# More exponentials moved from ScalarE to VectorE: a cheaper polynomial, its exponent bits on GpSimd, and a searched plan

## The chip, the cores and the metric

The kernel runs on one core of one Trainium2 chip. The metric is the device time of one execution in microseconds. All quoted runs are in the fast state unless said otherwise; executions of one kernel agree within 0.7%, those of e4 below within 1.1%. Names: PE is TensorE (matmul), PEld its weight load, ACT is ScalarE, DVE is VectorE, POOL is GpSimd. SBUF is the on-chip memory for operands, PSUM the one for TensorE's results. The *granted clock* is the share of full speed at which TensorE was allowed to run, as the profile records it.

## The reference

Two attention branches over the same `x` (2048 x 512, 32 heads of 16) are mixed by a gate. Branch A is softmax attention, branch B linear attention with softmax features.

```python
scores = jnp.einsum("bhqd,bhkd->bhqk", q, k) * (Dh ** -0.5)
p = softmax(scores)                       # 32 x 2048 x 2048 exponentials: this sets the time
a = (p @ v) @ wo
phi = concat(softmax(q @ w_phi), softmax(-q @ w_phi))   # branch B, small
b = (phi_q @ (phi_k^T v)) / (phi_q @ sum(phi_k)) @ wo
out = g * a + (1 - g) * b                 # g = sigmoid(x . gate_w)
```

Branch A's exponentials are cut into 2048 *units* of 128 x 512 (128 keys, 512 queries, one head). ScalarE does most of them. Some are done on VectorE, four units (four heads, one key tile) at a time: a *pack*.

## The kernel before

The program orders itself when it is built: every instruction is an `Op` with an engine, a duration, a priority and an earliest time, and a list scheduler turns them into one fixed order per engine. On the chip each engine runs its list in order and waits on semaphores. So "the plan" below means these fixed orders.

The work is 32 stretches of four heads and 512 queries. How many packs each gives to VectorE, and which key tiles they are:

```python
DVE_COUNT = (1, 2, 1, 1, 1, 2, 1, 2, 2, 1, 2, 2, 1, 2, 2, 2, 1, 2, 2, 1, 2, 2, 2, 1, 2, 2, 2, 1, 2, 3, 2, 2)   # 54
def dve_tiles(n):
    return ((6,), (5, 11), (4, 8, 12))[DVE_COUNT[min(n, NN - 1)] - 1]
```

The main chain on ScalarE takes three and two units at a time out of a ring of five PSUM banks:

```python
o_exp = s.op("act", w * 0.434 + 0.045, lambda e: e.activation(ET[:, s0:s0 + w, :], ps_ring[:, b0:b0 + w, :], ACT.Exp, scale=...))
```

A pack on VectorE writes `x*log2(e)` in fixed point (16 bits of fraction), then builds the bits of the bfloat16 result: 128 times the fixed-point number plus a correction, a polynomial in the fraction.

```python
rel = a + (z - a) * (j / nj) - 14 if n else a + 6     # when the pack's scores may be made
pr = rel + 12                                         # its priority
for i in range(4):      # scores into one of two PSUM banks, then a conversion out of it
    m = s.op("pe", ...matmul(self.bk(b), kT, qT))
    ws.append(s.op("dve", 0.605, ...tensor_scalar(EW[.., i], self.bk(b), EC, 127 * 65536, op0=mult, op1=add)))
f  = tensor_scalar(Ef, low_half(EW), 2.0 ** -16)      # f16 fraction, strided read
m1 = tensor_scalar(Em, Ef, 1.0, subtract)
t  = tensor_scalar(Et, Ef, 128 * EB, 128 * (EA - EB / 2), mult, add)
u  = tensor_tensor(Em, Ef, Em, mult)
g_ = tensor_tensor(Et, Et, Em, mult)
for hf in range(2):     # merge: reads the int32 words again
    scalar_tensor_tensor(ED[.., hf], in0=EW[.., hf], scalar=2.0 ** -9, in1=Et[.., hf], mult, add)
# ... TensorE then multiplies ED by V into the same accumulator as ScalarE's units
```

The softmax here doesn't subtract the row's maximum and nothing guards it: scores larger than these inputs give would overflow.

## Time and profile before

The time is 896.4 us (median of three runs; 895.56 to 900.07). The profiled run spans 897.3 us.

| what | us | read from |
|---|---|---|
| ACT busy | 864.0 (96%) | busy line |
| main exponentials | 837.9, 1832 units | costliest groups |
| DVE busy | 753.3 (84%) | busy line |
| first main exponential starts | 12.26 | timeline of ACT |
| last one ends, to the end | 9.3 | trace, records of ACT |
| gaps of ACT between the two | 13.7 | trace, records of ACT |

The first fence has lines of the profile page of the kernel before: busy time by engine (share of the span, instruction count), the chain of work that ended last, and three of the costliest groups (line, engine, operation, output and input, count | busy us, mean ns of one | idle time just before them).

```profile
PE 777.6 (87%) x5515; PEld 216.1 (24%) x5515; DVE 753.3 (84%) x1062; ACT 864.0 (96%) x801; POOL 7.0 (1%) x11
...
ACT 85%; PE 9%; DVE 3%; SPq 2%; DMA 0%; issue 0%; ACTq 0%
...
L691 ACT ACTIVATE ET<-ps_ring 128x1536 bf16<-128x1536 f32 (+1 forms) x733 | 837.9, 1331 | 15.5 <-PE ps_ring L674 8.0
...
L768 DVE TENSOR_SCALAR EW<-ps_mp 128x512 int32<-128x512 f32 x216 | 143.2, 681 | 45.6 <-PE ps_mp L764 44.7
...
L783 DVE SCALAR_TENSOR_TENSOR ED<-EW,Et 128x1024 uint16<-128x1024 int32 x108 | 126.3, 1210 | 0.3
```

ScalarE is the limit: it is busy 96% of the span and is 85% of the chain. VectorE has room: 45.6 us of its idle time lies before the conversions. The two merges of a pack are its dearest part: 126.3 us over 54 packs is 2.34 us per pack.

What one unit costs is read from the chain where it runs undisturbed. These are pieces of it (start, us, what):

```profile
466.85 22.60 ACT ET L691 x20
490.43 22.60 ACT ET L691 x20
```

Twenty instructions of three and two units alternating are 50 units, so a unit costs 22.60 / 50 = 0.452 us.

### The profile page before, as it was taken

To read this page: it belongs to the slowest core of one execution; us is meant where nothing else is said; L and a number is where in the kernel's file an instruction comes from. 1 tells how busy PE (TensorE), PEld (TensorE's weight loads), DVE (VectorE), ACT (ScalarE), POOL (GpSimd) and SP (SyncE) were. 2 spreads that over 40 slices of the span, in tenths; PEclk is the share of its full clock that TensorE was granted. 3 is DMA by queue.
4 is the path that set the end of the run, shared out by engine and by line. 5 is a ranking of instruction groups with operands and counts; after the bars stand their busy time and mean duration, and the time that the engine had idled before them with its cause. 6 is when DMAs were issued, how large, how long until landed. Compare 5 with 4: busy or idle time off the path is not lost.

```text
span 897.3 us, 13165 instructions
## 1 busy us (share of the span) xinstructions
PE 777.6 (87%) x5515; PEld 216.1 (24%) x5515; DVE 753.3 (84%) x1062; ACT 864.0 (96%) x801; POOL 7.0 (1%) x11
## 2 busy tenths in 40 slices
PE   7999998988888888888989888898888889887885
PEld 2223322222221222222222222222222222211221
DVE  3787878989994999699796897899979898889985
ACT  5998999999999999999999999999999999999985
POOL 3000000000000000000000000000000000000000
PEclk9999999999999999999999999999999999999998
DMA  5231000000000000000000000000000000000000
GB/s 111 55 76 49 1 7 3 2 4 4 4 4 1 4 4 4 4 1 10 10 10 10 4 7 10 10 7 8 1 4 4 10 10 13 6 1 4 4 1 24
DMA packets 25114, 11.21 MB, mean 12 GB/s; under 512 B 18016, under 2 KB 25056, under 8 KB 25056
## 3 DMA queue, kind: packets, MB, share of 16 engines
q1 hardware_dynamic: 23472, 9.99, 4.2%
q8 instruction: 43, 0.70, 0.3%
q10 hardware_dynamic: 1584, 0.39, 0.2%
q14 instruction: 15, 0.12, 0.0%
HBM read 3.16 MB, written 2.10 MB: 6 GB/s over the span
## 4 chain that ended last, share of the span: by engine, by line
ACT 85%; PE 9%; DVE 3%; SPq 2%; DMA 0%; issue 0%; ACTq 0%
ACT ET L691 82%; PE ps_ring L674 4%; ACT phi L913 3%; PE ps_mp L992 2%; SPq L501 2%; PE ps_ot L719 1%; PE ps_mp L561 1%; DVE ED L783 1%; DVE Em L778 0%; DVE EW L768 0%; PE ps_mp L764 0%; DMA xT<-in_A_x_dram 0%; DVE Ef L773 0%; DVE Et L779 0%; DVE Em L775 0%
## 5 line engine op out<-in xcount | busy, mean ns | idle before, releaser
L691 ACT ACTIVATE ET<-ps_ring 128x1536 bf16<-128x1536 f32 (+1 forms) x733 | 837.9, 1331 | 15.5 <-PE ps_ring L674 8.0
L674 PE MATMUL ps_ring<-qT,kT 64*128 64x512 bf16 x1832 | 365.8, 387 | 99.3 <-ACT ET L691 92.0
L768 DVE TENSOR_SCALAR EW<-ps_mp 128x512 int32<-128x512 f32 x216 | 143.2, 681 | 45.6 <-PE ps_mp L764 44.7
L719 PE MATMUL ps_ot<-ET,Vaug 128*17 128x512 bf16 x1832 | 177.4, 387 | 1.2 <-ACT ET L691 0.7
L674 PEld LDWEIGHTS ps_ring<-qT,kT 64*128 64x128 bf16 x1832 | 75.7, 93 | 334.6 <-ACT ET L691 301.9
L783 DVE SCALAR_TENSOR_TENSOR ED<-EW,Et 128x1024 uint16<-128x1024 int32 x108 | 126.3, 1210 | 0.3
L764 PE MATMUL ps_mp<-qT,kT 128*128 128x512 bf16 x216 | 79.8, 391 | 3.2 <-DVE EW L768 1.3
L719 PEld LDWEIGHTS ps_ot<-ET,Vaug 128*17 128x17 bf16 x1832 | 42.5, 87 | 139.5 <-issue 125.8
L773 DVE TENSOR_SCALAR Ef<-EW 128x2048 f16<-128x2048 uint16 x54 | 65.5, 1213 | 1.0
L778 DVE TENSOR_TENSOR Em<-Ef,Em 128x2048 f16<-128x2048 f16 x54 | 65.8, 1219 | 0.0
L779 DVE TENSOR_TENSOR Et<-Et,Em 128x2048 f16<-128x2048 f16 x54 | 65.5, 1212 | 0.3
L917 DVE TENSOR_REDUCE fsum<-phi 128x64 f32<-128x1024 bf16 x32 | 38.9, 1215 | 17.1 <-ACT phi L913 17.0
L736 PE MATMUL ps_ot<-zero,iden 128*32 128x512 bf16 (+2 forms) x288 | 47.7, 389 | 0.0
L561 PE MATMUL ps_mp<-Wp,xT 128*128 128x512 bf16 x128 | 40.3, 385 | 0.0
L561 PE MATMUL ps_mp<-xT,WA 128*128 128x512 bf16 x128 | 39.0, 385 | 1.1 <-DMA xT<-in_A_x_dram 1.1
L919 DVE TENSOR_TENSOR phi<-phi,frec 128x1024 bf16<-128x1024 bf16 x32 | 38.9, 1215 | 0.2
L913 ACT ACTIVATE phi<-ps_mp 128x512 bf16<-128x512 f32 x64 | 37.8, 699 | 0.0
L775 DVE TENSOR_SCALAR Em<-Ef 128x2048 f16<-128x2048 f16 x54 | 36.8, 681 | 0.9
L776 DVE TENSOR_SCALAR Et<-Ef 128x2048 f16<-128x2048 f16 x54 | 37.0, 685 | 0.0
L764 PEld LDWEIGHTS ps_mp<-qT,kT 128*128 128x128 bf16 x216 | 19.9, 96 | 53.5 <-issue 20.9
L802 DVE STREAM_TRANSPOSE T_80<-ps_ot 128x512 f32<-128x512 f32 x32 | 22.6, 708 | 8.1 <-PE ps_ot L719 8.1
L618 DVE CAST Vaug<-ps_mp 128x128 bf16<-128x128 f32 (+1 forms) x32 | 13.2, 424 | 14.2 <-PE ps_mp L561 14.1
(69 smaller groups left out, 405.7 us busy)
## 6 DMA issues: line engine op xcount, KB each, us to landing
out_dram<-outt SPq DMA_DIRECT2D x16, 128.0 KB, 1.7
qT<-qst SPq DMA_DIRECT2D x120, 16.0 KB, 1.8
WA<-in_A_wqkv_dram SPq DMA_DIRECT2D x3, 384.0 KB, 4.6
WBV<-in_B_wqkv_dram SPq DMA_DIRECT2D x1, 512.0 KB, 5.4
WoA<-in_A_wo_dram SPq DMA_DIRECT2D x1, 512.0 KB, 3.8
WoB<-in_B_wo_dram SPq DMA_DIRECT2D x1, 512.0 KB, 4.6
WA<-in_A_wqkv_dram ACTq DMA_DIRECT2D x3, 128.0 KB, 3.4
xT<-in_A_x_dram SPq DMA_TRANSPOSE x16, 2.7
```

The lines of the kernel that those rows point to most:

```text
L561: m = s.op("pe", self.c_mm(n), lambda e, c=c: e.matmul(self.bk(b)[:, 0:n], lhs(c), rhs(c), start=(c == 0), stop=(c == 3)), deps if c == 0 ...
L674: return lambda e: e.matmul(self.ps_ring[:, x % RING, :], self.kT[r, g // 2, kt * P:(kt + 1) * P], self.qT[r, n % 2, i, :], start=True, st ...
L691: self.o_exp.append(s.op("act", w * 0.434 + 0.045, lambda e, b0=b0, s0=s0, w=w: e.activation(self.ET[:, s0:s0 + w, :], self.ps_ring[:, b0: ...
L719: return lambda e: e.matmul(self.ps_ot[32 * i:32 * i + VSL, :], self.Vaug[:, kt, h, :], self.ET[:, (4 * p + k) % NSLOT, :], start=(kt == 0 ...
L736: return lambda e: e.matmul(self.ps_ot[c:c + nc, :], self.iden[r:r + nr, 0:nc], self.zero[r:r + nr, :], start=False, stop=False, tile_posi ...
L764: m = s.op("pe", self.c_mm(512), lambda e, i=i, b=b: e.matmul(self.bk(b), self.kT[:, cp, kt * P:(kt + 1) * P], self.qT[:, n % 2, i, :], st ...
L768: ws.append(s.op("dve", 0.605, lambda e, i=i, b=b: e.tensor_scalar(self.EW[:, ew.idx, i * QCH:(i + 1) * QCH], self.bk(b), float(EC), float ...
L773: f = s.op("dve", 1.13, lambda e: e.tensor_scalar(self.Ef[:], lo(), float(2.0 ** -16), None, op0=ALU.mult), ws + [self.ed_prev], pr)
L778: u = s.op("dve", 1.13, lambda e: e.tensor_tensor(self.Em[:], self.Ef[:], self.Em[:], ALU.mult), [m1], pr)
L779: g_ = s.op("dve", 1.13, lambda e: e.tensor_tensor(self.Et[:], self.Et[:], self.Em[:], ALU.mult), [t, u], pr)
L783: vs.append(s.op("dve", 1.12, lambda e, c0=c0: e.scalar_tensor_tensor(out=self.ED[:, ed.idx, c0], in0=self.EW[:, ew.idx, c0], scalar=float ...
L913: ex.append(s.op("act", 0.478, lambda e, sg=sg: e.activation(self.phi[:, ph.idx, :, sg, :], self.bk(b).rearrange("p (h f) -> p h f", f=DH) ...
```

## The change

The intent: make a pack cheaper for VectorE, so that it can take more packs, 65 instead of 54. The polynomial becomes a cubic about the middle of the fraction (d = f - 0.49985); its constant part is the integer 53. The exponent bits, `128 * high_half + 53`, are made by GpSimd. One 16-bit addition replaces the two int32 merges. GpSimd and VectorE can get into each other's way at the SBUF, so the plan gets two new notions: a `port` flag on VectorE instructions that it keeps apart from GpSimd's pass, and a `gate` that releases the pass of one pack only at the first or second PSUM conversion of a later one. All leads, paces and bounds are replaced by searched numbers. Three smaller edits are in the diff too: up to four packs per stretch instead of three, the score matmuls of successive packs kept in order, and a higher priority (`LEAD[2]`) for VectorE instructions that free one of the scarce PSUM banks.

```diff
+LEAD = [16.9408, 8.9394, 19.7683, 21.1253, 20.1566]
+PACE = [7.9948, 0.4589]
+BOUNDS = [5.8136, 10.5124, 10.0461, 26.2873]
-EA, EB = 0.34370964, 0.07826797
+EM = 53
+EPHI = 0.49984589
+E1, E2, E3 = 125.48413, 43.840203, 9.9574722
-DVE_COUNT = (1, 2, 1, 1, 1, 2, 1, 2, 2, ...)    # 54
+DVE_COUNT = (1, 1, 1, 2, 2, 2, 2, 1, 3, ...)    # 65
 ... (scheduler: a gated GpSimd op is parked until a gate op starts on VectorE; it then waits for the op before that one)
+            if e == "dve":
+                while o.gate and parked:
+                    c = parked.pop(0)
+                    c.war.append(last)
 ... (in the pack)
-        rel = a + (z - a) * (j / nj) - 14 if n else a + 6
-        pr = rel + 12
+        rel = a + (z - a) * (j / nj) - LEAD[0] if n else a + 6
+        pr = rel + LEAD[1]
+        h = s.op("pool", 1.9, lambda e: e.tensor_scalar(
+            out().bitcast(dt.int16), half(1, dt.int16), 128.0, float(EM), op0=ALU.mult, op1=ALU.add), ws, pr, gate=...)
-        f, m1, t, u, g_ and two scalar_tensor_tensor merges
+        f = tensor_scalar(Ef, half(0), 2.0 ** -16, -EPHI, mult, add)      # port
+        t = tensor_scalar(Em, Ef, E3, E2, mult, add)                      # port
+        u = tensor_tensor(Em, Ef, Em, mult)                               # port
+        q = tensor_scalar(Em, Em, E1, add)                                # port
+        g_ = tensor_tensor(Em, Ef, Em, mult)                              # port
+        vs = [tensor_tensor(out(), out().bitcast(int16), Em, add)]        # port; waits for h
 ... (port flags on three instructions outside the packs; LEAD, PACE, BOUNDS in place of the old constants)
```

More of the change, by code (lines that the diff above doesn't have):

```diff
@@ L28 @@
 PASSES = 1
+LEAD = [16.9408, 8.9394, 19.7683, 21.1253, 20.1566]
+PACE = [7.9948, 0.4589]
+BOUNDS = [5.8136, 10.5124, 10.0461, 26.2873]
 VSL = 17
 EC = 0.25 * 1.4426950408889634 * 65536
-EA, EB = 0.34370964, 0.07826797
-DVE_COUNT = (1, 2, 1, 1, 1, 2, 1, 2, 2, 1, 2, 2, 1, 2, 2, 2, 1, 2, 2, 1, 2, 2, 2, 1, 2, 2, 2, 1, 2, 3, 2, 2)
+EM = 53
+EPHI = 0.49984589
+E1, E2, E3 = 125.48413, 43.840203, 9.9574722
+DVE_COUNT = (1, 1, 1, 2, 2, 2, 2, 1, 3, 2, 1, 3, 1, 2, 3, 1, 2, 3, 2, 2, 2, 2, 3, 2, 1, 3, 2, 2, 4, 1, 3, 3)
 def dve_tiles(n):
-    return ((6,), (5, 11), (4, 8, 12))[DVE_COUNT[min(n, NN - 1)] - 1]
+    return ((6,), (5, 11), (4, 8, 12), (3, 6, 9, 12))[DVE_COUNT[min(n, NN - 1)] - 1]
 class Buf:
@@ L66, with __init__ @@
     __slots__ = ("eng", "dur", "fns", "deps", "prio", "rel", "alloc", "frees", "nleft", "users", "start", "end",
-                 "ready", "seq", "dma", "order", "inc", "tick", "clock", "war", "cols", "lat", "cfg", "exp", "grp")
-    def __init__(self, eng, dur, fns, deps, prio, rel, alloc, frees, dma, order, cols=0, cfg="F"):
+                 "ready", "seq", "dma", "order", "inc", "tick", "clock", "war", "cols", "lat", "cfg", "exp", "grp", "port",
+                 "gate", "go")
+    def __init__(self, eng, dur, fns, deps, prio, rel, alloc, frees, dma, order, cols=0, cfg="F", port=False,
+                 gate=False):
         self.cols = cols
+        self.port = port or eng == "pool"
+        self.gate = gate
+        self.go = False
         self.cfg = cfg
@@ L104, in op @@
     def op(self, eng, dur, fns, deps=(), prio=0.0, rel=0.0, alloc=(), frees=(), dma=0, order=(),
-           cols=0, cfg="F"):
+           cols=0, cfg="F", port=False, gate=False):
         if not isinstance(fns, (list, tuple)):
@@ L109, in op @@
             cols = 90
-        o = Op(eng, dur, list(fns), deps, prio, rel, alloc, frees, dma, order, cols, cfg)
+        o = Op(eng, dur, list(fns), deps, prio, rel, alloc, frees, dma, order, cols, cfg, port, gate)
+        if eng == "dve" and any(getattr(b.pool, "scarce", False) for b in o.frees):
+            o.prio -= LEAD[2]
         self.ops.append(o)
@@ L154, in run @@
         cfg = "F"
+        hold = {"dve": 0.0, "pool": 0.0}
+        parked, last = [], None
         self.at = 0
@@ L182, in run @@
                     best = (s, e)
+            if best is None and parked:
+                c = parked.pop(0)
+                c.go = True
+                heapq.heappush(future["pool"], (max(t.values()), c.seq, c))
+                continue
             assert best is not None, "scheduler is stuck"
@@ L210, in run @@
                         continue
+                if e == "pool" and c.gate and not c.go:
+                    parked.append(c)
+                    continue
+                if e == "dve" and c.port and hold["pool"] > now + 0.02 and len(held) < 8:
+                    held.append(it)
+                    continue
                 o = c
                 break
+            if e == "pool" and o is None:
+                continue
+            if e == "dve" and o is None and held:
+                o = held[0][2]
+                held = held[1:]
             if o is None:
@@ L238, in run @@
                 o.war.extend(war)
+            if o.port:
+                other = "dve" if e == "pool" else "pool"
+                now = max(now, hold[other])
+                hold[e] = now + o.dur
+            if e == "dve":
+                while o.gate and parked:
+                    c = parked.pop(0)
+                    c.go = True
+                    if last is not None:
+                        c.war.append(last)
+                    heapq.heappush(future["pool"], (now + self.TAIL["dve"], c.seq, c))
+                last = o
             o.start = now
@@ L419, in memory @@
         at("Em", [P, 4 * QCH], dt.float16)
-        at("Et", [P, 4 * QCH], dt.float16)
         at("ED", [P, 2, 4 * QCH], dt.uint16)
@@ L439, in pools @@
         self.mp = BufPool(2)
+        self.mp.scarce = True
         self.qst_p = BufPool(2)
@@ L468, in program @@
     def program(self):
-        self.T0 = 11.0
-        self.ut = 0.481
+        self.T0, self.ut = PACE
         self.loads()
@@ L570, in emit_qT @@
         n0 = qc * NG + 2 * cp
-        dl = self.tn(n0) - (14.0 if n0 else 2.0)
+        dl = self.tn(n0) - (LEAD[4] if n0 else 2.0)
         st = Buf(self.qst_p, 8 if n0 == 0 else 2)
@@ L580, in emit_qT @@
                     self.qT[:, n, i, :], self.qst[:, st.idx, :], self.par[:, n, i:i + 1], None, op0=ALU.mult),
-                    [o_ev, self.o_par, self.o_qz[n]], dl + 6 * n, 12 * n, frees=[st]) for i in ORDER]
+                    [o_ev, self.o_par, self.o_qz[n]], dl + 6 * n, 12 * n, frees=[st], port=True) for i in ORDER]
         self.st_q[n0 // 2] = (st, o_ev)
@@ L594, in place_qT @@
             "sp", 0.24, [put(i) for i in range(4)],
-            [o_ev, self.qk_last.get(n - 2), self.qk_dve.get(n - 2), self.o_qz[par]], self.tn(n) - 14.0, dma=65536,
+            [o_ev, self.qk_last.get(n - 2), self.qk_dve.get(n - 2), self.o_qz[par]], self.tn(n) - LEAD[4], dma=65536,
             frees=[st])]
@@ L633, in main_chain @@
             pos.append(pos[-1] + 64 - 4 * len(dve_tiles(n)))
-        self.ed_prev = None
+        self.ed_prev = self.eq_prev = None
         self.units = units
@@ L756, in dve_pack @@
         a, z = self.tn(n), self.tn(n + 1)
-        rel = a + (z - a) * (j / nj) - 14 if n else a + 6
-        pr = rel + 12
+        rel = a + (z - a) * (j / nj) - LEAD[0] if n else a + 6
+        pr = rel + LEAD[1]
         ew, ed = Buf(self.EW_p, 2), Buf(self.ED_p, 1)
         ws = []
-        m = None
+        m = self.eq_prev
         for i in range(4):
@@ L769, in dve_pack @@
                 self.EW[:, ew.idx, i * QCH:(i + 1) * QCH], self.bk(b), float(EC), float(127 * 65536),
-                op0=ALU.mult, op1=ALU.add), [m], pr, frees=[b]))
-            self.qk_dve[n] = m
-        lo = lambda: self.EW[:, ew.idx, :].bitcast(dt.uint16).rearrange("p (n two) -> p n two", two=2)[:, :, 0]
-        f = s.op("dve", 1.13, lambda e: e.tensor_scalar(self.Ef[:], lo(), float(2.0 ** -16), None, op0=ALU.mult),
-                 ws + [self.ed_prev], pr)
-        m1 = s.op("dve", 0.6, lambda e: e.tensor_scalar(self.Em[:], self.Ef[:], 1.0, None, op0=ALU.subtract), [f], pr)
@@ L776, in dve_pack @@
-        t = s.op("dve", 0.6, lambda e: e.tensor_scalar(
-            self.Et[:], self.Ef[:], float(128 * EB), float(128 * (EA - EB / 2)), op0=ALU.mult, op1=ALU.add), [f], pr)
-        u = s.op("dve", 1.13, lambda e: e.tensor_tensor(self.Em[:], self.Ef[:], self.Em[:], ALU.mult), [m1], pr)
-        g_ = s.op("dve", 1.13, lambda e: e.tensor_tensor(self.Et[:], self.Et[:], self.Em[:], ALU.mult), [t, u], pr)
-        vs = []
-        for hf in range(2):
-            c0 = slice(hf * 2 * QCH, (hf + 1) * 2 * QCH)
-            vs.append(s.op("dve", 1.12, lambda e, c0=c0: e.scalar_tensor_tensor(
-                out=self.ED[:, ed.idx, c0], in0=self.EW[:, ew.idx, c0], scalar=float(2.0 ** -9), in1=self.Et[:, c0],
-                op0=ALU.mult, op1=ALU.add), [g_], pr, alloc=[ed] if hf == 0 else (), frees=[ew],
-                order=vs[-1:]))
+                op0=ALU.mult, op1=ALU.add), [m], pr, frees=[b], gate=i < 2))
@@ new lines, in dve_pack @@
+            self.qk_dve[n] = self.eq_prev = m
+        half = lambda k, t: self.EW[:, ew.idx, :].bitcast(t).rearrange("p (n two) -> p n two", two=2)[:, :, k]
+        out = lambda: self.ED[:, ed.idx, :]
+        h = s.op("pool", 1.9, lambda e: e.tensor_scalar(
+            out().bitcast(dt.int16), half(1, dt.int16), 128.0, float(EM), op0=ALU.mult, op1=ALU.add), ws, pr,
+            alloc=[ed], frees=[ew], gate=(n, j) != (NN - 1, nj - 1))
+        f = s.op("dve", 1.13, lambda e: e.tensor_scalar(
+            self.Ef[:], half(0, dt.uint16), float(2.0 ** -16), -EPHI, op0=ALU.mult, op1=ALU.add),
+            ws + [self.ed_prev], pr, frees=[ew], port=True)
@@ new lines, in dve_pack @@
+        t = s.op("dve", 0.6, lambda e: e.tensor_scalar(
+            self.Em[:], self.Ef[:], E3, E2, op0=ALU.mult, op1=ALU.add), [f], pr, port=True)
+        u = s.op("dve", 1.13, lambda e: e.tensor_tensor(self.Em[:], self.Ef[:], self.Em[:], ALU.mult), [t], pr, port=True)
+        q = s.op("dve", 0.6, lambda e: e.tensor_scalar(self.Em[:], self.Em[:], E1, None, op0=ALU.add), [u], pr, port=True)
+        g_ = s.op("dve", 1.13, lambda e: e.tensor_tensor(self.Em[:], self.Ef[:], self.Em[:], ALU.mult), [q], pr, port=True)
@@ L787, in dve_pack @@
+        vs = [s.op("dve", 1.13, lambda e: e.tensor_tensor(out(), out().bitcast(dt.int16), self.Em[:], ALU.add), [g_, h], pr,
+                   port=True)]
         self.ed_prev = vs[-1]
@@ L809, in norm @@
             self.rinv[:, j, :, None].to_broadcast([P, 16, DH]), ALU.mult),
-            [rc, self.o_onTA.get((n - 2) // 2) if j == 0 else None], pr)
+            [rc, self.o_onTA.get((n - 2) // 2) if j == 0 else None], pr, port=True)
         if j == 0:
@@ L857, in branch_b @@
                     self.bk(b).rearrange("p (c j) -> p c j", c=4)), 512, r + 8)
-        k0, k1 = tn(3.4), tn(12.4)
-        q0, q1 = tn(13), tn(28)
+        k0, k1 = tn(BOUNDS[0]), tn(BOUNDS[1])
+        q0, q1 = tn(BOUNDS[2]), tn(BOUNDS[3])
         self.o_onTB, self.b_onTB = {}, {}
@@ L867, in branch_b @@
             b, m = self.proj(lambda c, t=t: self.xT[:, c, t * P:(t + 1) * P], lambda c: self.WBV[:, c, :], D,
-                             [self.d_wbv], r + 18, r + 4, 1, [vb])
+                             [self.d_wbv], r + 18, r + 4 - LEAD[3], 1, [vb])
             o_vb = s.op("dve", self.c_v(512), lambda e, b=b, vb=vb: e.tensor_copy(
@@ L909, in feature @@
         b, m = self.proj(lambda c: self.xT[:, c, t * P:(t + 1) * P], lambda c: self.Wp[:, c, D * qk:D * qk + D], D,
-                         [self.o_wp[(qk, jc)] for jc in range(4)], r + 5, r, 2, [ph, fs])
+                         [self.o_wp[(qk, jc)] for jc in range(4)], r + 5, r - LEAD[3], 2, [ph, fs])
         ex = []
@@ L920, in feature @@
             flat(), flat(), self.frec[:, fs.idx, :, None].to_broadcast([P, 64, DH]), ALU.mult), [rc], r + 10,
-            frees=[fs])
+            frees=[fs], port=True)
         return ph, sc
```

## The prediction

> **What bounds the kernel now.** ScalarE. The page's busy line gives ACT 864.0 of 897.3 us (96%), DVE 753.3 (84%), PE 777.6, POOL 7.0 (1%); the chain that ended last is 85% ACT, 82% the main exponentials. Those are 1832 units of 128x512, run in groups of three and two. In undisturbed stretches of the chain twenty instructions (50 units) take 22.60 us: 0.452 us per unit. The remaining 33 us of the span: 10 to 12 us before the first main exponential (it starts at 12.26), about 9 us after the last, and some 12 us of gaps between, where ACT waits for scores or for a product (the waits view: 8.0 and 6.8 us, part of it at the start).
>
> **What the change does.**
> - Offloaded packs 54 to 65: 11 x 4 = 44 units leave ScalarE. 44 x 0.452 = 19.9 us, all on the critical engine.
> - VectorE per pack, before, by starts of successive instructions in the timeline: four PSUM conversions about 2.5 us, the strided fraction 1.13, two short passes 1.2, two products 2.26, two int32 merges 2.24: about 9.4. After: 2.5 + 1.13 + 0.6 + 1.13 + 0.6 + 1.13 + one 16-bit add 1.13, about 8.2. The total goes from 54 x 9.4 = 508 to 65 x 8.2 = 533 us. VectorE then is busy about 780 us, near 89% of a shorter span; it must idle less, and can: much of its idle time is work not yet released.
> - GpSimd gets 65 passes over 2048 elements. An estimate from its 128x2048 fill in this trace (1874 ns) is 1.9 us each, about 125 us, off the chain. The danger is the port: the Trainium skill, "SBUF — State Buffer", Who interferes with whom, says that a VectorE instruction in a 2-port mode or with two SBUF inputs and a GpSimd instruction block each other whole, while one with at most one SBUF input outside these modes does not contend. This trace cannot show it: GpSimd works only at the start. The change releases each pass at the start of a later pack's PSUM conversions (about 2.5 us, longer with interleaved waits), so 1.9 us should fit. I expect 0 to 0.3 us lost per pack, under 20 us of VectorE time, mostly absorbed in its idle time.
> - TensorE: about 4 us more, not critical.
> - The new leads and bounds may recover a few us of the 12 us of gaps; a fuller VectorE may cost the same. I count zero.
>
> **Prediction.** 896.4 - 19.9 = 876.5; I say 876 us, 80% range 864 to 889. Faster by over 2% (below 878.5) 0.58, within 2% 0.39, slower 0.03.
>
> **What would show it.** Right: ACT busy about 844 us, 1788 units at an unchanged 0.452, chain still over 80% ACT; first and last exponentials' margins unchanged; ACT idle in the middle 5 to 20 us; DVE busy 770 to 800; POOL about 130 us, its passes near 1.9 us and inside conversions; no VectorE pass lengthened by more than 0.1 us in the mean. Wrong on the port: passes on GpSimd of 3 us or more, or products and short passes visibly lengthened beside them, and ACT waiting for scores or products by 20 us and more. Wrong on the plan: DVE above 93%, pack products late, the score chain held by late PSUM conversions.
>
> **What would make it wrong.** GpSimd takes 3 us or drifts off its slot, so that VectorE loses about 1 us per pack (65 us) and becomes the limit: the time stays near 890. Only two PSUM banks serve the conversions, projections and outputs; if they queue, ACT gaps grow. Or the search closes nearly all gaps: near 864.

## The result, and the profile after

The changed kernel took 872.11 us (median of 4; 870.81 to 872.99) beside 898.11 us before (median of four, one run more than above); the ratio is 0.9711 (95% interval 0.9677 to 0.9745). Ratios in this text are the mean time of one kernel's runs over that of the other's in the same rounds, so they are not quite the ratio of the medians. Executions over 1.5% slower than the fastest of the same kernel are left out of the means.

The lines of the changed kernel's page that answer to those above, with the new pass on GpSimd:

```profile
PE 748.0 (86%) x5242; PEld 215.5 (25%) x5330; DVE 796.9 (91%) x1118; ACT 842.7 (97%) x783; POOL 131.5 (15%) x76
...
ACT 93%; PE 4%; DVE 1%; SPq 1%; DMA 1%; issue 0%; another core or an unknown queue 0%
...
L735 ACT ACTIVATE ET<-ps_ring 128x1536 bf16<-128x1536 f32 x715 | 817.5, 1346 | 10.8 <-PE ps_ring L718 9.2
...
L819 POOL TENSOR_SCALAR ED<-EW 128x2048 int16<-128x2048 int16 x65 | 124.4, 1915 | 717.4 <-DVE Em L829 101.5
L812 DVE TENSOR_SCALAR EW<-ps_mp 128x512 int32<-128x512 f32 x260 | 170.8, 680 | 11.7 <-PE ps_mp L808 9.0
...
L830 DVE TENSOR_TENSOR ED<-ED,Em 128x2048 uint16<-128x2048 int16 x65 | 81.3, 1251 | 0.5 <-POOL ED L819 0.2
```

ScalarE lost 21.3 us of work, VectorE gained 43.6 us and now idles little before its conversions (11.7 us instead of 45.6). The GpSimd pass takes 1915 ns; VectorE waited for its result for 0.2 us in all.

Taken from the records of ACT in the two traces, the span falls apart so:

| part of the span, us | before | after | difference |
|---|---|---|---|
| until the first main exponential | 12.26 | 14.92 | +2.7 |
| ACT busy from then to the last | 862.1 | 840.8 | -21.3 |
| ACT gaps from then to the last | 13.7 | 5.9 | -7.8 |
| after the last | 9.3 | 9.5 | +0.2 |
| span | 897.3 | 871.1 | -26.2 |

So there is more than the packs: the gaps shrank, and the start came later.

### The profile page after: what moved, and what is told of

Same layout as the page of the kernel before. It is cut to its first block, busy times and chain, and to the rows that moved or that the text cites. A ratio compares the mean times of both kernels' runs of the same rounds, so it can differ in the third digit from the quotient of the medians.

```text
span 871.1 us, 12869 instructions
## 1 busy us (share of the span) xinstructions
PE 748.0 (86%) x5242; PEld 215.5 (25%) x5330; DVE 796.9 (91%) x1118; ACT 842.7 (97%) x783; POOL 131.5 (15%) x76
## 4 chain that ended last, share of the span: by engine, by line
ACT 93%; PE 4%; DVE 1%; SPq 1%; DMA 1%; issue 0%; another core or an unknown queue 0%
ACT ET L735 90%; ACT phi L958 4%; PE ps_ring L718 2%; PE ps_mp L605 1%; SPq L545 1%; PE ps_ot L763 1%; DMA xT<-in_A_x_dram 0%; DVE kvbd L938 0%; DMA out_dram<-outt 0%; DVE outt L1070 0%; DVE fsum L962 0%; DVE EW L812 0%; PE ps_ot L836 0%; DVE T L847 0%; PE ps_mp L896 0%
## 5 line engine op out<-in xcount | busy, mean ns | idle before, releaser
L735 ACT ACTIVATE ET<-ps_ring 128x1536 bf16<-128x1536 f32 x715 | 817.5, 1346 | 10.8 <-PE ps_ring L718 9.2
L718 PE MATMUL ps_ring<-qT,kT 64*128 64x512 bf16 x1788 | 357.1, 387 | 95.9 <-ACT ET L735 88.9
L819 POOL TENSOR_SCALAR ED<-EW 128x2048 int16<-128x2048 int16 x65 | 124.4, 1915 | 717.4 <-DVE Em L829 101.5
L812 DVE TENSOR_SCALAR EW<-ps_mp 128x512 int32<-128x512 f32 x260 | 170.8, 680 | 11.7 <-PE ps_mp L808 9.0
L718 PEld LDWEIGHTS ps_ring<-qT,kT 64*128 64x128 bf16 x1788 | 73.7, 93 | 300.2 <-ACT ET L735 260.2
L808 PE MATMUL ps_mp<-qT,kT 128*128 128x512 bf16 x221 | 83.2, 388 | 4.4 <-DVE EW L812 1.0
L822 DVE TENSOR_SCALAR Ef<-EW 128x2048 f16<-128x2048 uint16 x65 | 83.3, 1282 | 0.5
L830 DVE TENSOR_TENSOR ED<-ED,Em 128x2048 uint16<-128x2048 int16 x65 | 81.3, 1251 | 0.5 <-POOL ED L819 0.2
L829 DVE TENSOR_TENSOR Em<-Ef,Em 128x2048 f16<-128x2048 f16 x65 | 81.1, 1247 | 0.5
L827 DVE TENSOR_TENSOR Em<-Ef,Em 128x2048 f16<-128x2048 f16 x65 | 79.3, 1220 | 0.4
L825 DVE TENSOR_SCALAR Em<-Ef 128x2048 f16<-128x2048 f16 x65 | 49.2, 757 | 0.4
L828 DVE TENSOR_SCALAR Em<-Em 128x2048 f16<-128x2048 f16 x65 | 47.3, 728 | 0.4
L808 PEld LDWEIGHTS ps_mp<-qT,kT 128*128 128x128 bf16 x260 | 24.0, 96 | 64.0 <-issue 31.6
L847 DVE STREAM_TRANSPOSE T<-ps_ot 128x512 f32<-128x512 f32 x32 | 22.7, 710 | 6.7 <-PE ps_ot L763 6.2
```

The source lines that it names most:

```text
L718: return lambda e: e.matmul(self.ps_ring[:, x % RING, :], self.kT[r, g // 2, kt * P:(kt + 1) * P], self.qT[r, n % 2, i, :], start=True, st ...
L735: self.o_exp.append(s.op("act", w * 0.434 + 0.045, lambda e, b0=b0, s0=s0, w=w: e.activation(self.ET[:, s0:s0 + w, :], self.ps_ring[:, b0: ...
L808: m = s.op("pe", self.c_mm(512), lambda e, i=i, b=b: e.matmul(self.bk(b), self.kT[:, cp, kt * P:(kt + 1) * P], self.qT[:, n % 2, i, :], st ...
L812: ws.append(s.op("dve", 0.605, lambda e, i=i, b=b: e.tensor_scalar(self.EW[:, ew.idx, i * QCH:(i + 1) * QCH], self.bk(b), float(EC), float ...
L819: h = s.op("pool", 1.9, lambda e: e.tensor_scalar(out().bitcast(dt.int16), half(1, dt.int16), 128.0, float(EM), op0=ALU.mult, op1=ALU.add) ...
L822: f = s.op("dve", 1.13, lambda e: e.tensor_scalar(self.Ef[:], half(0, dt.uint16), float(2.0 ** -16), -EPHI, op0=ALU.mult, op1=ALU.add), ws ...
```

## The experiments

The theory to be tested (S): the gain is units taken off ScalarE at 0.45 us each, plus smaller gaps from the new plan; the cheaper pack only makes the room. The rival (V): VectorE was holding up the chain, and its relief is the gain. A second question is what the GpSimd pass costs through the shared SBUF port. "Gaps" are always ACT's, between the first and the last main exponential.

### The parts of the change one by one

**e1: the new pack, but 54 packs on the old plan.** Counts, leads, pace and bounds are the old ones; the gate and the port rule stay.

```diff
-LEAD = [16.9408, 8.9394, 19.7683, 21.1253, 20.1566]; PACE = [7.9948, 0.4589]; BOUNDS = [5.8136, 10.5124, 10.0461, 26.2873]
+LEAD = [14.0, 12.0, 0.0, 0.0, 14.0]; PACE = [11.0, 0.481]; BOUNDS = [3.4, 12.4, 13.0, 28.0]
-DVE_COUNT = ...   # 65
+DVE_COUNT = ...   # the 54 of before
```

> The new arithmetic and the GpSimd pass, but 54 packs on the old plan (old counts, leads, pace and bounds). Theory S (the gain is units taken off ScalarE, plus smaller gaps from the plan; a cheaper pack on VectorE is only what makes room): ScalarE busy stays near 864 us and the time within 1% of before, 888 to 898, although VectorE falls to about 690 to 705 us. Rival V (VectorE was holding the chain, its relief is the gain): 880 us or less, with ScalarE gaps after the first exponential down from 13.7 us to under 6.

Measured: 902.11 us, ratio to before 1.0039 (1.0014 to 1.0064). The busy line of its page:

```profile
PE 786.1 (87%) x5469; PEld 219.7 (24%) x5469; DVE 707.6 (79%) x1008; ACT 864.3 (96%) x801; POOL 110.5 (12%) x65
```

VectorE does 45.7 us less than before and the kernel is no faster (the figure for VectorE is a little above what I expected, the gaps are 16.6 us). Theory V falls in this form: on the old leads the cheaper pack alone buys nothing. (The 707.6 us contain 10.9 us of the lengthening beside GpSimd that is explained below.)

**e1b: the changed kernel with the 54 old counts**, leads, pace and bounds new.

```diff
-DVE_COUNT = ...   # 65
+DVE_COUNT = ...   # the 54 of before
```

> The changed kernel with the old 54-pack counts and all else new, leads, pace and bounds too. Theory S: ScalarE busy 864, the time 885 to 892: it keeps the smaller gaps (about 8 us) but not the 20 us of the 44 units. If it comes under 878, the number of packs is not what carries the gain. If it is at 896 or more, the plan carries nothing without its counts.

Measured: 892.97 us, ratio 0.9956 (0.9935 to 0.9977), a microsecond above the range. In its trace (its fastest run, 889.71 us, with a granted clock of 0.995 where the others had 0.985 to 0.989) ACT is busy 860.6 us between the first and last exponential, the gaps are 3.9 us and the first exponential starts at 14.07. So the gaps are about 10 us smaller than before and the start is 2 us later; by the medians the time gains 5 us. Beside e1, from which it differs in leads, pace and bounds alone, the median falls by 9.1 us and the gaps from 16.6 to 3.9 us, some of it perhaps through this run's higher clock (e1's profiled run had 0.982). The busy line of e1b's page:

```profile
PE 777.0 (88%) x5462; PEld 218.3 (25%) x5462; DVE 719.4 (81%) x1008; ACT 862.5 (97%) x801; POOL 109.5 (12%) x65
```

From here to the changed kernel ACT's work falls by 860.6 - 840.8 = 19.8 us, 0.45 us for each of the 44 units, and the time falls by 892.97 - 872.11 = 20.9 us (medians of different rounds). Both halves of theory S hold where the new pack is used. The old pack with 54 packs on a newly searched plan was not run, so how far the gaps would have shrunk without the cheaper pack stays open.

**e2: 65 packs with the old polynomial**, all on VectorE, nothing on GpSimd. The plan of the changed kernel does not fit it (the scheduler deadlocks on buffers), so I searched a plan for it with the scheduler's own end time as the goal.

```diff
-        h = pool pass; f, t, u, q, g_, one tensor_tensor
+        f, m1, t, u, g_ and two scalar_tensor_tensor merges, as before
-DVE_COUNT, LEAD, PACE, BOUNDS of the change
+DVE_COUNT (also 65), LEAD, PACE, BOUNDS searched anew
```

> 65 packs with the old quadratic on VectorE alone, no GpSimd, on a plan searched for it anew (its own counts, leads and bounds). Theory S with VectorE as the limit of how much can be offloaded: VectorE would need 753 + 11 x 9.4 = 857 us, 97% or more of the span; ScalarE busy falls to 843 as in the changed kernel but its gaps grow, 878 to 895. If it reaches 874 or less, the cheaper pack was not needed and the searched plan alone carries the gain.

Measured: 887.79 us, ratio 0.9883 (0.986 to 0.9905).

```profile
PE 776.8 (88%) x5476; PEld 218.1 (25%) x5476; DVE 842.5 (95%) x1183; ACT 843.0 (95%) x783; POOL 7.0 (1%) x11
```

ScalarE has as little work as in the changed kernel (843.0 us), but VectorE is at 842.5 us, the gaps are 14.5 us, and 16.6 us follow the last exponential instead of 9.5. The same 65 packs are worth 10 us instead of 26: the cheaper pack is needed for the rest. A longer search might find a better plan for this variant; that stays open.

**e3: the changed kernel with its 65 counts but the old leads, pace and bounds.**

```diff
-LEAD, PACE, BOUNDS of the change
+LEAD = [14.0, 12.0, 0.0, 0.0, 14.0]; PACE = [11.0, 0.481]; BOUNDS = [3.4, 12.4, 13.0, 28.0]
```

> The changed kernel with its 65-pack counts but the old leads, pace and bounds. If the searched plan is needed for the gain: 895 to 930, with ScalarE busy 843 as in the changed kernel and its gaps 40 us or more. If the units alone decide: 872 to 880.

Measured: 926.52 us, ratio 1.0321 (1.03 to 1.0341), slower than before. The busy line of e3's page, then its waits view (engine, what waited, for what: us in total, times, the longest):

```profile
PE 793.7 (86%) x5632; PEld 223.9 (24%) x5632; DVE 802.4 (87%) x1118; ACT 844.0 (91%) x783; POOL 131.1 (14%) x76
```

```profile
ACT ET L735 <- PE ps_ot L763: 44.9, 11, 17.6
```

ScalarE's work is right, yet it waits 44.9 us for products (`ps_ot`), once for 17.6 us; its gaps are 53 us. VectorE is not the reason as an average (87%). But look at the longest wait in the windows view (length, then busy us and count of PE, PEld, DVE, ACT and POOL):

```profile
817.72:835.30 17.58, 12.24 (x59) 3.95 (x58) 17.41 (x20) 0.00 (x0) 3.79 (x2) 1.00 0.02 5
```

VectorE is busy for nearly all of it with one pack after another, and the product that ScalarE waits for stands in TensorE's list behind the products of two of these packs (L836). So the order of the lists is the reason, here at least. With the new pack, four kernels make a square: 54 packs take 902.1 us on the old leads and 893.0 on the new, 65 packs take 926.5 and 872.1. Neither the arithmetic nor the counts carry the gain without the plan.

**e5: the new cubic, 65 packs, exponent bits on VectorE**, again on a plan searched for it.

```diff
-        h = s.op("pool", 1.9, lambda e: e.tensor_scalar(
+        h = s.op("dve", 1.13, lambda e: e.tensor_scalar(
-            ... pr, frees=[b], gate=i < 2))
+            ... pr, frees=[b]))
```

> 65 packs, the same cubic, but the exponent-bit pass runs on VectorE instead of GpSimd, on a plan searched for it anew. VectorE gains 65 passes of about 1.2 us and loses the 21 us of lengthening: about 850 us busy. If VectorE's load is what limits the offload: ScalarE busy 843 as in the changed kernel, gaps and tail grow, 878 to 892, like the old arithmetic at 65 packs. If moving the pass to GpSimd was not needed: 869 to 875.

Measured: 882.84 us, ratio 0.9849 (0.982 to 0.9878); VectorE busy 840.5 us, gaps 15.5 us.

```profile
PE 754.9 (86%) x5305; PEld 216.7 (25%) x5388; DVE 840.5 (95%) x1183; ACT 843.3 (96%) x783; POOL 7.0 (1%) x11
```

Of the gain of 26 us about 11 hang on having that one pass on another engine, under the same reservation about the plan.

### What GpSimd and VectorE do to each other

The Trainium skill ("SBUF — State Buffer", Who interferes with whom) says that a VectorE instruction in a 2-port mode contends with GpSimd, and one with two SBUF inputs with a GpSimd instruction that reads SBUF, as this pass does; the one that issues first holds the shared ports for its whole instruction and the other waits. The timeline of the changed kernel agrees. First VectorE near 500 us, then the GpSimd pass there (start, us, engine, line, operation):

```profile
499.88 0.68 DVE L812 TENSOR_SCALAR EW<-ps_mp 128x512 int32<-128x512 f32 x1
500.48 2.54 DVE L830 TENSOR_TENSOR ED<-ED,Em 128x2048 uint16<-128x2048 int16 x1
502.94 0.68 DVE L812 TENSOR_SCALAR EW<-ps_mp 128x512 int32<-128x512 f32 x1
...
500.05 1.90 POOL L819 TENSOR_SCALAR ED<-EW 128x2048 int16<-128x2048 int16 x1 [11.02 <-DVE Em L829]
```

The pass begins 0.17 us into a conversion, as the gate wants. The 16-bit addition starts 0.43 us after the pass did and takes 2.54 us instead of its median 1.22: it ends 1.07 us after the pass has ended. The conversions beside it keep their length. The wait is *inside* the recorded duration of the addition, so it counts as busy and no waits view shows it. Going through the records, I find 27 VectorE instructions more than 0.15 us longer than their group's median, every one beside a GpSimd pass, 20.9 us in all; with one single instruction told of below it is 22.2 us, 0.34 us per pack. In the kernel before there is none.

**e4: no gate and no port flags.** The pass may start as soon as its own pack is converted.

```diff
-        self.port = port or eng == "pool"
-        self.gate = gate
+        self.port = False
+        self.gate = False
```

> The changed kernel, but the GpSimd pass is not held back for a later conversion and the plan no longer keeps two-port VectorE passes apart from it: it may start as soon as its own pack's conversions are done. If the two engines exclude each other (theory P): the lengthening of VectorE passes beside GpSimd passes, 21 us in 27 instructions in the changed kernel, rises to 60 to 120 us, VectorE goes past 850 us busy and the time to 885 to 915. If the placement is a nicety (rival): lengthening under 40 us, time 869 to 877.

Measured: 944.85 us, ratio 1.0546 (1.0491 to 1.06); VectorE is busy 849.7 us. Sixty-one VectorE instructions are lengthened, all beside a pass, by 72.5 us in all. The passes are blocked as well, as their mean shows:

```profile
L819 POOL TENSOR_SCALAR ED<-EW 128x2048 int16<-128x2048 int16 x65 | 162.2, 2495 | 748.3 <-DVE EW L812 649.0 <-PE ps_ot L836 99.2
```

The lengthening is in the expected range, but the time is 30 us above the range I gave: it rose by 73 us over the changed kernel for 52 us more of lengthening. The waits views, here of e4 and then of the changed kernel, show how VectorE's delay gets to ScalarE:

```profile
ACT ET L735 <- PE ps_ring L718: 70.3, 89, 4.7
...
PEld ps_mp L808 <- DVE EW L812: 43.9, 73, 2.3
```

```profile
PEld ps_mp L808 <- DVE EW L812: 14.9, 49, 0.8
...
ACT ET L735 <- PE ps_ring L718: 9.2, 5, 4.9
```

The pack's score matmuls (L808) wait for a PSUM bank that a late conversion still holds, in TensorE's one queue, so the main chain's scores (L718) behind them wait too. The mean granted clock of TensorE fell from 0.99 to 0.94 as well. How much of the 73 us is the clock and how much the queue is not separated. Nor is the port alone: without gate and flags the scheduler makes another plan, and 848 of the 1118 places in VectorE's list hold another instruction than in the changed kernel (the two traces compared place by place). In e7 all 1118 are the same.

**e7: the pass twice per pack**, first into a scratch tile, with the same order on VectorE. The pass then also waits for the one before it, to keep the scratch tile free of races.

```diff
-        h = s.op("pool", 1.9, lambda e: e.tensor_scalar(out()..., half(1)...), ws, pr,
+        h = s.op("pool", 1.9, [lambda e: e.tensor_scalar(self.Ex[:], half(1)...),
+            lambda e: e.tensor_scalar(out()..., half(1)...)], ws + [self.h_prev], pr,
```

> The changed kernel with the GpSimd pass done twice per pack (first into a scratch tile), 3.8 us instead of 1.9, the VectorE order unchanged. Theory P (a two-port or two-input VectorE pass waits until the GpSimd pass has ended): nearly every pack now collides, lengthening 100 to 180 us, 890 to 940. Rival (GpSimd is off the path with 717 us idle, so its length is free): 869 to 877.

Measured: 946.05 us, ratio 1.0547 (1.0517 to 1.0576). GpSimd has 645.5 us of idle time before these passes and still costs the kernel 74 us. Seventy VectorE instructions are lengthened by 61 us, less than the 100 to 180 us I expected, while the time is above my range: again the loss grows on its way (granted clock 0.95, gaps 65 us). But the port is not the only way here. The longer pass also finishes too late, and VectorE's addition waits for its result, as the waits view says:

```profile
DVE ED L833 <- POOL ED L821: 23.4, 17, 2.2
```

In the changed kernel this wait is 0.2 us. How the 74 us divide between lengthening, lateness and clock is not shown. What e7 does show is that the length of a pass on an idle engine is not free.

**e8: a pass that only writes.** It is replaced by a fill with a constant. Its output is wrong, which doesn't matter for the time.

```diff
-        h = s.op("pool", 1.9, lambda e: e.tensor_scalar(out()..., half(1)...), ws, pr,
+        h = s.op("pool", 1.9, lambda e: e.memset(out().bitcast(dt.int16), 16256), ws, pr,
```

> Wrong results on purpose: the GpSimd pass is replaced by a fill of the same tile with a constant, which reads nothing; order and releases unchanged. If the read side is what two-input passes contend for, the lengthened two-input tensor passes (9 of 27 instructions, about 8 us with the single one on the key-value product) fall to none, while the short and strided one-input passes (18, about 13 us) stay lengthened; total lengthening 10 to 16 us. If any GpSimd access blocks any two-port pass, both kinds stay, near 21 us. Time within 1% of the changed kernel either way.

Measured: one run, 867.62 us (state unknown). The lines of VectorE's addition in e8 and in the changed kernel (minimum/median/maximum in ns):

```profile
L829 DVE TENSOR_TENSOR ED<-ED,Em x65: 1162/1216/1226, 37.2 to 851.3; 128x2048 uint16<-128x2048 int16 x65
...
L824 DVE TENSOR_SCALAR Em<-Ef x65: 631/684/1562, 30.8 to 847.3; 128x2048 f16<-128x2048 f16 x65
```

```profile
L830 DVE TENSOR_TENSOR ED<-ED,Em x65: 1160/1215/2541, 39.4 to 858.2; 128x2048 uint16<-128x2048 int16 x65
...
L825 DVE TENSOR_SCALAR Em<-Ef x65: 627/683/1680, 32.9 to 854.2; 128x2048 f16<-128x2048 f16 x65
```

No two-input instruction is lengthened any more (the maximum fell from 2541 to 1226 ns); the one-input short pass still is (1562 ns). In all 18 remain, 10.7 us; the nine two-input ones and the key-value product are gone, as expected. The fill takes 1805 ns at the mean instead of 1915, too small a difference to explain this. The same section of the skill says that two SBUF inputs contend with a GpSimd instruction that reads SBUF and not with one that only writes it. That the one-input passes still lengthened run in a 2-port mode is inferred from this and not seen in the trace.

### A late start and one collision on the chain

Two things in the changed kernel's trace looked repairable. The first is the start. Its timeline on TensorE, with the idle time before an entry and what ended it in brackets:

```profile
12.74 1.07 PE L605 MATMUL ps_mp<-xT,WA 128*128 128x512 bf16 x3 [2.13 <-DMA xT<-in_A_x_dram]
13.61 0.31 PE L605 MATMUL ps_mp<-WA,xT 128*128 128x128 bf16 x1
13.86 1.46 PE L718 MATMUL ps_ring<-qT,kT 64*128 64x512 bf16 x5
```

A projection that needs the second block of `x` lies in front of the first scores and waits 2.13 us for the DMA. In this run TensorE's clock record also has half clock from 13.15 to 19.98 us, which c0's profiled run below has not. The second is near 322 us. The key-value product of branch B (`kvbd`, two SBUF inputs) was not given a port flag. It starts beside a pass and takes 2.00 us; TensorE waits (the bracket names the conversion that the product had held up on VectorE), and so does ScalarE, twice. Lines of the changed kernel's timeline:

```profile
320.45 1.90 POOL L819 TENSOR_SCALAR ED<-EW 128x2048 int16<-128x2048 int16 x1 [10.65 <-DVE kvacc L934]
...
320.89 2.00 DVE L938 TENSOR_TENSOR kvbd<-kvacc,m 128x512 bf16<-128x512 f32 x1
...
323.65 0.24 PE L990 MATMUL ps_mp<-kvbd,phiT 128*128 128x68 bf16 x2 [1.57 <-DVE EW L812]
...
324.89 5.11 ACT L735 ACTIVATE ET<-ps_ring 128x1536 bf16<-128x1536 f32 x4 [1.58 <-PE ps_ring L718]
...
331.10 2.37 ACT L735 ACTIVATE ET<-ps_ring 128x1536 bf16<-128x1536 f32 x2 [1.10 <-PE ps_ring L718]
```

Four kernels were run in five rounds on one chip. **c0 is the changed kernel again**, as the control (no edit).

> The changed kernel itself, as the control of this series: 870 to 874, ratio near 0.971.

Measured: 871.3 us, ratio to before 0.9708 (0.9695 to 0.9721). Its trace has the same two gaps (1.56 and 1.17 us); its start wait is 1.87 us and its first exponential starts at 14.09.

**f1: the projection is released later**, behind the first scores.

```diff
-                         QCH, [self.d_wk[cp], self.d_x[j]], dl - 2, dl - 25, 1)
+                         QCH, [self.d_wk[cp], self.d_x[j]], dl - 2, max(dl - 25, 12.8) if cp == 0 and j == 1 else dl - 25, 1)
```

> The changed kernel with one edit: the second key projection, which needs the second block of x, is not released to TensorE before 12.8 us of the plan's time, so that it queues behind the first scores instead of in front of them. If that projection's wait for its data (2.1 us in front of the first scores) is what delays the first main exponential from 12.3 to 14.9 us: it starts at about 12.5 again, and the time falls by 1.5 to 2.7 us against the control. If the start does not carry through (later data limits the first stage anyway): under 0.7 us.

Measured: 873.49 us, ratio 0.9731 (0.9718 to 0.9744): 0.2% slower than the control, a miss. The first exponential does start at 12.61, but see TensorE next:

```profile
14.14 0.60 PE L718 MATMUL ps_ring<-qT,kT 64*128 64x512 bf16 x3
...
18.17 0.44 PE L718 MATMUL ps_ring<-qT,kT 64*128 64x512 bf16 x2 [3.43 <-DMA xT<-in_A_x_dram]
```

Between these two lines TensorE's list has one matmul of the next block's projection (its record is missing), and the queue stands for 3.43 us until that block has landed. The plan expects every block too early: it reckons 0.84 us for the issue of a transposing load, where the trace has 1.26. ScalarE's fifth exponential starts at 21.33, in the control's trace at 19.07: 2.3 us later, about the 2.2 us by which the medians differ. (The changed kernel's first profiled run, the one with half clock at the start, has it at 21.27.) Moving one item moved the wait, and made it longer.

**f9: f1, and the one pass near 320 us also waits for the key-value product.** The order on every engine stays.

```diff
+                bd, bz = self.kvd        # the two key-value products
+                late = [o for o in self.s.out if o.eng == "pool" and o.start < bd.end and bd.start < o.end]
+                for o in late:
+                    o.war.append(bz)     # and o is placed behind bz in the list of all engines
```

> As f1_start_floor, and one GpSimd pass, the one beside the key-value product near 320 us, waits until that product is done; the order of the instructions on every engine stays. If the collision there (the product took 2.00 us instead of 0.69) made the two ScalarE gaps of 1.6 and 1.1 us that follow: they go, and the time falls by another 1.5 to 2.7 us against f1_start_floor, to about 866 to 868. If the gaps have another cause they stay, and the two kernels are within 0.7 us.

Measured: 870.2 us, ratio 0.9689 (0.9676 to 0.9702), 3.3 us below f1, a little more than expected; in absolute terms it is 2 us above my 866 to 868, because f1 gained nothing. The product takes 0.68 us, and both gaps are gone. The windows view of the changed kernel, then of f9 (busy us and instruction count of each engine; PEclk is TensorE's granted clock):

```profile
320.00:327.00 7.00, 5.23 (x31) 1.42 (x31) 6.43 (x13) 5.33 (x6) 1.90 (x1) 0.77 0.04 11
327.00:334.00 7.00, 6.64 (x37) 1.64 (x37) 5.83 (x12) 5.82 (x6) 0.00 (x0) 0.74 0.00 1
```

```profile
320.00:327.00 7.00, 5.42 (x46) 1.57 (x46) 7.00 (x16) 7.00 (x7) 1.90 (x1) 1.00 0.05 13
327.00:334.00 7.00, 6.66 (x52) 2.18 (x49) 7.00 (x11) 6.96 (x7) 0.00 (x0) 1.00 0.00 1
```

The columns after the length are PE, PEld, DVE, ACT, POOL, PEclk, DMA share and GB/s. One collision of 1.3 us cost 1.7 and 1.1 us of ScalarE's busy time in the two windows, and the mean granted clock fell to about three quarters for both. The clock record of the changed kernel has one stretch at half clock across the two, from 323.76 to 330.59 us, where f9 has none. The windows view of it:

```profile
323.76:330.59 6.83, 6.46 (x40) 1.71 (x40) 5.09 (x13) 4.95 (x4) 0.00 (x0) 0.50 0.01 4
```

The Trainium skill ("TensorE: Matmul & The Clock Gate", What's actually happening) gives half clock as TensorE's state after at least one idle window of about 3.4 us. The halving is seen here, and 6.83 us is two such windows; a wholly idle window is not seen. In the 3.41 us before the drop TensorE was busy for 1.84 us by its records, whose ends are modelled, and its longest pause was 1.57 us.

**f7: 66 packs, the start edit, port flags on the key-value products, and a plan searched anew.**

```diff
+        ... ALU.mult), [acc[0], acc[1], self.o_m4], r, r, port=True)     # both products; and the edit of f1
-DVE_COUNT, LEAD, PACE, BOUNDS of the change
+DVE_COUNT (66), LEAD, PACE, BOUNDS searched anew
```

> 66 packs, the start edit, the key-value product kept apart from the GpSimd passes in the plan, and a plan searched anew. If a unit is worth 0.452 us wherever it goes: ScalarE busy 841 us, gaps 3 to 8 us, 864 to 870. If VectorE, now near 805 us of busy time, has reached its limit: gaps over 10 us, 872 or more.

Measured: 865.99 us, ratio to before 0.9645 (0.963 to 0.9661); against the control of the same rounds 0.9645 / 0.9708 = 0.9935.

```profile
PE 747.9 (87%) x5296; PEld 217.1 (25%) x5382; DVE 806.7 (93%) x1128; ACT 840.4 (97%) x782; POOL 133.7 (15%) x77
```

It beats both kernels. ACT's work falls by 2.3 us, as one pack more should give with some noise, its gaps are 3.9 us and its first exponential starts at 12.28 and runs on. VectorE at 93% is not yet the limit. The plan differs as a whole, so the remaining 3 us are not assigned to a single cause.

## Why the prediction was right, and where it was off

It was right: 876 us predicted, range 864 to 889, measured 872.1, "faster" as the likelier class. The mechanism held: units left the critical engine at about the stated pace. The closeness of the number is in part luck, as the last lines of this section show.

- *"44 x 0.452 = 19.9 us, all on the critical engine."* Held. ACT's busy time fell to 842.7 us (844 predicted); e1b to the changed kernel gives 19.8 us of work and 20.9 us of time for exactly these 44 units. (Before to after, all of ACT's work fell by 21.3 us, the main exponentials by 20.4.)
- *"VectorE ... about 780 us"*, 770 to 800 in the list of signs. It was 796.9. The pack is cheaper by about what was costed: e1 saves 45.7 us net over 54 packs, and 10.9 us of lengthening was added, so 56.6 / 54 = 1.05 us per pack against the predicted 1.2.
- *"1.9 us each, about 125 us, off the chain."* 1915 ns and 124.4 us. The estimate from a fill of the same size was good.
- *"0 to 0.3 us lost per pack, under 20 us."* It was 0.34 us and 22 us, a little over. *"No VectorE pass lengthened by more than 0.1 us in the mean"* held for the groups (the short pass: 685 to 757 ns), but a mean was the wrong thing to look at: single instructions took 1.3 us more, and one of them, the unflagged key-value product, stood on the chain and cost about 3 us (f9 against f1).
- *"TensorE: about 4 us more."* Not seen. Its busy time fell from 777.6 to 748.0 us, mostly because the plan puts fewer filler matmuls on a tile of zeros (288 before, 101 after; 47.7 and 19.4 us).
- *"The new leads and bounds may recover a few us ... a fuller VectorE may cost the same. I count zero."* This is the mis-sized term. The gaps went from 13.7 to 5.9 us, and e1 against e1b shows that with the new pack the leads do that at the old counts as well (16.6 to 3.9 us). e3 shows the other face of it: with the old leads the 65 packs would have lost 28 us. A change that replaces every lead and bound by a searched number should have got more than zero for that.
- *"First and last exponentials' margins unchanged."* Wrong for the first: it came 2.7 us later in the profiled run and 1.8 us later in c0's. In both, a projection in front of the first scores waits for `x` (2.13 and 1.87 us), which the plan expected earlier than it lands; the rest in the profiled run goes with its half clock. This took back a third of the gap's gain, and f1 shows that it is not got back by moving that one item.

Together the two missed terms are -7.8 + 2.7 = -5.1 us, which is about the distance between 876 and 872. That they partly cancel is luck, and so is the base: the prediction started from 896.4 us, while the four runs of the result have 898.11. The gain itself was 26.0 us where 19.9 were counted.

## What to carry to other kernels

When the critical engine is almost always busy, count the work that leaves it and multiply by its undisturbed pace: that gave about three quarters of this gain (19.9 of 26.2 us), and relief on an engine beside it gave nothing without a new plan (e1). To have another engine take that work, its list must be in the right order; an average of 87% busy can hide 45 us of waiting (e3). When two engines share a port, look for single lengthened instructions rather than raised means, place the intruder beside work that does not use the port, and flag every instruction that does, the one-off ones too.

## What the Trainium skill lacked or had wrong

- "SBUF — State Buffer", Who interferes with whom, is right on all points tried here (e8, a single run, separates reads from writes), but does not say that the blocked VectorE instruction shows the wait as its own busy time: 2.54 us instead of 1.22, counted as busy, in no waits view. 22 of the changed kernel's 796.9 busy microseconds are such waits.
- "Perfetto Trace Analysis", Optimizing Scalar/DVE Operations, says that offloading between VectorE and GpSimd might not help because of the shared port. Here it helped by 11 us (e5 882.84, the change 872.11, each on its own searched plan), given conversions out of PSUM to hide beside; without that placement, in another order, the kernel was 73 us slower (e4).
- "GPSIMD Engine Reference", Engine selection, calls one-input passes roughly line-rate, and the page has a model of cycles per element, but no measured time for this form. The runs show 1.897 us at the median for 2048 int16 elements per partition, multiply and add, read with a 4-byte step.
- No page that I read names the way a delay grows: a lengthened VectorE instruction of 1.3 us held up TensorE's queue, its clock was at half for 6.83 us without a wholly idle window before, and ScalarE lost about 3 us.
